# Products with the hidden-axis matrix spread over the running round, and stores handed to the DMA queue three ticks later

## The chip, the cores and the metric

The kernel runs on one core of a Trainium2 chip. The metric is the device time of one execution in microseconds (us), the median of several runs. The engines are called as the profile calls them: PE (matmuls) with PEld (its weight loads), DVE (vector), ACT (scalar), POOL (GpSimd), and SP, which here only issues DMAs.

## The reference

Two layers, each a spectral block and an attention block, on x of 2048 x 640 in float32. What the change touches is the spectral block:

```python
def _A_ref(x, dft_seq_re, dft_seq_im, dft_hid_re, dft_hid_im):
    a = einsum("bsd,ed->bse", x, dft_hid_re)
    b = einsum("bsd,ed->bse", x, dft_hid_im)
    return einsum("ts,bse->bte", dft_seq_re, a) - einsum("ts,bse->bte", dft_seq_im, b)

x = x + _A_ref(layernorm(x), ...)      # spectral
x = x + _B_ref(layernorm(x), ...)      # sliding-window attention, 32 heads, window 256
x = x + _A_ref(layernorm(x), ...)
x = x + _B_ref(layernorm(x), ...)
```

So each spectral block normalizes the rows, multiplies them with a 640-wide complex matrix (here `whid`), and multiplies the result with a 2048 x 2048 complex matrix (here `cmat`).

## The kernel before

Every float32 operand is split into a high and a low float16 part, and a product of two numbers is three matmuls (high x high, high x low, low x high). ACT writes a high part, DVE or POOL the low one, as the difference.

`spectral(layer, ...)` does one spectral block in four rounds (`NR = 4`). A round takes 512 of the 2048 input rows, in four tiles of 128 (`RS = 4`). For each of those tiles `z_stage(s)` forms the product with `whid`, which is called a whid stage here: four products of 15 matmuls each, every one into a bank of PSUM named `pf`, of which there are two (`new_f`, `bufs=2`). A bank is free again when DVE's subtractions (`minus`, L257) have read it. From the four products `parts`, `scaled` and `minus` make seven operands, kept in a buffer `zc` (or `early` for the first two stages of rounds 0 and 2).

Then the main part of the round: eight tiles of output (`j` = 0 to 7, `NJ = 8`), for each of which seven products (a Strassen-like scheme) of 12 matmuls are formed in banks `x`, `y` and `z`. `main_a(r, j)` does the first, `main_b(r, j)` four, `main_c(r, j)` the last two, which come after `main_a` of the next `j`. Their sums go into rows `res`, which are loaded (from the input in round 0, from `accd` in DRAM later) and stored to `accd`, or to `x2d` in the last round. DVE adds most of them from PSUM (`add`, L512); POOL adds three 320-column halves out of a work tile `pf` (L526, L536, L547). Four buffer pairs make `res` (`bufs=4`, two tiles of output).

The left operands come from `cmat`: `load_c` fetches one 1 MB block `cq` per `j`, two `j` ahead, `take_c` forms four sums `cs` on POOL (L478 to L481), and seven operands `cc` are split one per tick: `high` on ACT (L486), `low` on DVE (L489).

After each product stands a `tick()`: it emits the next pair of `splits` and one step of every generator in the list `side`. Such generators are `side_norm(s)` (load, normalize and split 128 rows of x for a whid stage of the next round, first layer only), `turn_x(s)` (transposes of those rows on PE), `b_max` (in round 0: 20 maxima on DVE, L618) and `b_split` (rounds 1 and 2: 15 chunks of the attention's weights, scaled on ACT, split on ACT and POOL at L660 to L663, stored to `bwd`). In the second layer the transposed rows are fetched from DRAM instead (`hidden.fetch`).

The stages of the next round stand partly inside the running one: after j = 6 and j = 7 stages 0 and 1; stages 2 and 3 follow at the start of the next round. `Projections()` loads the attention's weights (`big<-bwd`, two halves of 2400 KB) once the last stage is done, since they use the buffer of `whid`.

Every engine executes its own instructions in the order in which the framework put them; SP's DMAs are all issued from one queue, and an issue that has to wait for a buffer or for data holds those behind it.

Of the kernel before, what the change touches and what calls it, by code (L numbers as in the profile page):

```python
# [49 lines left out]
TURN_STEPS = 8  # L50
NORM_STEPS = (4, 9)
ROW_STEPS = 3
X_UP = 2.0 ** 10
C_UP = 2.0 ** 8
W_UP = 2.0 ** 13
# [6 lines left out]
def body(ctx: ExitStack, tc: tile.TileContext, x_in, cmat, whid, wqkv, wo, out):  # L62
# [108 lines left out]
    def load(out, in_):  # L171
        with ExitStack() as order:
            if in_turn[0] and loads:
                order.enter_context(tc.issue_after(loads[-1]))
            i = nc.sync.dma_start(out, in_)
        loads.append(i.ins)
# [26 lines left out]
    class Hidden:  # L203
# [21 lines left out]
        def stage(self, s, pool, new=new_f):  # L225

            w, xt = self.w, self.xt(s)
            if s % 8 < 2:
                zc = new_early()[:, :14 * HD].rearrange("p (m a d) -> p m a d", m=7, a=2)
            else:  # L230
                zc = pool.tile([P, 7, 2, HD], F16, tag="zc", name="zc", bufs=4)
            self.zc[s] = zc
            b11, b12, t1, t2, t3, t4 = (self.zf[:, k] for k in range(6))
            z = None

            def product(c, n):
                nonlocal z
                z = new()
                cs = slice(n * HD, (n + 1) * HD)
                k = 0  # L240
                for dt in range(ND):
                    for l, r in ((0, 0), (0, 1), (1, 0)):
                        self.last = matmul(z[:, :HD], xt[:, l, dt], w[:, r, c, dt, cs],
                                                     start=k == 0, stop=k == 14).ins
                        k += 1
                        yield 136
                z = z[:, :HD]

            def parts(m, f):
                nc.scalar.activation(zc[:, m, 0], f, AF.Copy)  # L250
                nc.gpsimd.tensor_tensor(zc[:, m, 1], f, zc[:, m, 0], op=OP.subtract)

            def scaled(o):
                nc.scalar.activation(o, z, AF.Copy, scale=Z_DOWN)

            def minus(o, f):
                nc.vector.scalar_tensor_tensor(o, z, Z_DOWN, f, op0=OP.mult, op1=OP.subtract)  # L257

            yield from product(0, 0)
            scaled(zc[:, B11, 0])  # L260
            scaled(b11)
            minus(zc[:, B11, 1], zc[:, B11, 0])
            yield 0
            yield from product(0, 1)
            scaled(b12)
            minus(t1, b11)
            parts(T1, t1)
            yield 0
            yield from product(1, 1)
            scaled(zc[:, B22, 0])  # L270
            minus(t2, t1)
            minus(t3, b12)
            minus(zc[:, B22, 1], zc[:, B22, 0])
            parts(T2, t2)
            parts(T3, t3)
            yield 0
            yield from product(1, 0)
            scaled(zc[:, B21, 0])
            minus(zc[:, B21, 1], zc[:, B21, 0])
            minus(t4, t2)  # L280
            parts(T4, t4)
            yield 0
# [62 lines left out]
    def spectral(layer, res_src, hidden, first):  # L345
        with ExitStack() as st:
# [30 lines left out]
            def drain():  # L377
                while splits or side:
                    tick()

            def load_w(n):
                c, dt = divmod(n, ND)
                f = sb.tile([P, D], F32, tag="xin", name="wst", bufs=NXIN)
                load(f, whid[c, :, dt])
                return f
# [125 lines left out]
            def add(o, z, f):  # L511
                marks["dve"] = nc.vector.scalar_tensor_tensor(o, z, Y_DOWN, f, op0=OP.mult, op1=OP.add).ins  # L512
# [4 lines left out]
            def main_a(r, j):  # L517
                res = [keep.tile([P, D], F32, tag="res", name="res", bufs=4) for k in range(2)]
                for k in range(2):
                    load(res[k], res_src[2 * j + k] if r == 0 else acc_d[2 * j + k])  # L520
                f = sb.tile([P, 3, HD], F32, tag="pf", name="pf", bufs=2)
                x = new_bank("x")
                cc = CC.pop((r, j))
                z = product(r, x, cc, 0, True, False)
                marks["act"] = nc.scalar.activation(f[:, 0], z, AF.Copy, scale=Y_DOWN).ins
                nc.gpsimd.tensor_tensor(res[1][:, lo], res[1][:, lo], f[:, 0], op=OP.add)  # L526
                tick()
                state[r, j] = [res, f, cc, x]

            def main_b(r, j):  # L530
                (x0, x1), f, cc, x = state[r, j]
                p1, u2, u3 = (f[:, k] for k in range(3))
                y = new_bank("y")
                z = product(r, y, cc, 1, True, False)
                add(u2, z, p1)
                nc.gpsimd.tensor_tensor(x0[:, hi], x0[:, hi], u2, op=OP.add)  # L536
                tick()
                z = product(r, x, cc, 2, False, True)
                add(x0[:, lo], z, x0[:, lo])
                tick()  # L540
                zb = new_bank("z")
                z = product(r, zb, cc, 4, True, False)
                add(x1[:, hi], z, x1[:, hi])
                tick()
                z = product(r, y, cc, 3, False, False)
                add(u3, z, p1)
                nc.gpsimd.tensor_tensor(x1[:, hi], x1[:, hi], u3, op=OP.add)  # L547
                tick()
                state[r, j] = [(x0, x1), cc, y, zb]

            def main_c(r, j):
                res, cc, y, zb = state.pop((r, j))
                x0, x1 = res
                z = product(r, zb, cc, 6, False, True)
                add(x0[:, hi], z, x0[:, hi])
                tick()
                z = product(r, y, cc, 5, False, True)
                add(x1[:, lo], z, x1[:, lo])
                last = r == NR - 1
                for k in range(2):  # L560
                    load((x2_d if last else acc_d)[2 * j + k], res[k])
                if last and j == 0:
                    side.append(chain(finish(0, 1), finish(1, 1)))
                tick()
# [87 lines left out]
            def b_split(n0, n1):  # L652
                fs = {n: b_chunk(n) for n in range(n0, n0 + 3)}
                for _ in range(4):
                    yield 1
                for n in range(n0, n1):
                    f = fs.pop(n)
                    t = keep.tile([P, 2, D], F16, tag="xto", name="bst", bufs=2)
                    hi, lo, sc = t[:, 0], t[:, 1], wsc[:, 0:1]
                    nc.scalar.activation(f, f, AF.Copy, scale=sc)  # L660
                    nc.scalar.activation(hi, f, AF.Copy)
                    yield 1
                    nc.gpsimd.tensor_tensor(lo, f, hi, op=OP.subtract)  # L663
                    cs = slice((n % 3) * D, (n % 3 + 1) * D)
                    for k in range(2):
                        load(bw_d[k][:, n // 3, cs], t[:, k])
                    if n + 3 < n1:
                        fs[n + 3] = b_chunk(n + 3)
                    for _ in range(5):
                        yield 1  # L670
# [22 lines left out]
                side.append(hidden.rest)  # L693
            load_c(0)
            for r in range(NR):
                for k in range(0 if r == 0 else 2, RS):
                    s = RS * r + k
                    if first:
                        if s == 1:
# [13 lines left out]
                            take_c(0)  # L713
                    if first or s > 1:
                        z_stage(s)
                if r == NR - 1:
                    proj = Projections()
                for j in range(NJ):
# [9 lines left out]
                    if r == NR - 1 and j == NJ - 1:  # L728
                        for _ in early_qk:
                            pass  # L730
                        for k in (1, 0):
                            proj.stack[k] = new_stack()
                            fill_stack(proj.stack[k], 0, k)
                    if first:
                        if r < NR - 1 and j in (3, 4):
                            side.append(side_norm(RS * (r + 1) + j - 3))
                        if r < NR - 1 and j == 5:
                            turn_x(RS * (r + 1))
                    if j == 0 and r == 0:
                        with behind():  # L740
                            while splits:
# [4 lines left out]
                    with ExitStack() as order:  # L746
# [3 lines left out]
                        if j:  # L750
                            main_c(r, j - 1)
                        main_b(r, j)
                    if r < NR - 1 and j >= NJ - 2:
                        k = j - (NJ - 2)
                        s = RS * (r + 1) + k
                        if first:
                            turned_x(s)
                            turn_x(s + 1, 2 if k == 0 else 0)
                            side.append(side_norm(s + 2))
                        else:  # L760
                            hidden.fetch(s)
                        z_stage(s)
                main_c(r, NJ - 1)
                if r == NR - 1:
                    drain()
# [542 lines left out]
```

## Time and profile before

| what | value |
| --- | --- |
| median of 3 runs | 2232.29 us (2230.44 to 2234.39) |
| profiled execution: span | 2233.0 us (nothing is shown around the span) |
| mean granted clock of PE | 0.991 |
| PE busy | 2122.0 us, 95% |
| DVE busy | 1646.4 us, 74% |
| POOL busy | 1391.6 us, 62% |
| ACT busy | 1288.8 us, 58% |
| DMA | 292.96 MB, mean 131 GB/s |

The first layer's spectral rounds begin at 53.75, 189.90, 332.60 and 472.30 us of the trace; a steady round of the second layer lies between 1320.00 and 1444.20. In a row of the timeline stand start, duration, engine, line, operation, `out<-in`, the count, and in brackets the idle time before it with what ended it. SPq is SP issuing a DMA; the transfer itself takes longer.

### The profile page before, as it was taken

To read this page: it belongs to the slowest core of one execution; us is meant where nothing else is said; L and a number is where in the kernel's file an instruction comes from. 1 tells how busy PE (TensorE), PEld (TensorE's weight loads), DVE (VectorE), ACT (ScalarE), POOL (GpSimd) and SP (SyncE) were. 2 spreads that over 40 slices of the span, in tenths; PEclk is the share of its full clock that TensorE was granted. 3 is DMA by queue.
4 is the path that set the end of the run, shared out by engine and by line. 5 is a ranking of instruction groups with operands and counts; after the bars stand their busy time and mean duration, and the time that the engine had idled before them with its cause. 6 is when DMAs were issued, how large, how long until landed. Compare 5 with 4: busy or idle time off the path is not lost.

```text
span 2233.0 us, 55112 instructions
## 1 busy us (share of the span) xinstructions
PE 2122.0 (95%) x21985; PEld 1494.7 (67%) x21985; DVE 1646.4 (74%) x3577; ACT 1288.8 (58%) x2155; POOL 1391.6 (62%) x1788
## 2 busy tenths in 40 slices
PE   7999899899999999999899999999998999999998
PEld 4767566676666766677566777777675666677765
DVE  8887958767677887887858758585767777777664
ACT  5434455443467777777754443434434777777775
POOL 5775968758355665566446858586674555566443
PEclk9999999999999999999999999999999999999999
DMA  6664646455533422333424536364743323332231
GB/s 252 219 224 143 229 138 225 156 188 175 142 79 67 103 71 73 94 91 84 134 79 160 193 127 212 110 207 145 256 133 96 83 63 85 93 87 59 57 80 37
DMA packets 187607, 292.96 MB, mean 131 GB/s; under 512 B 13908, under 2 KB 120660, under 8 KB 178004
## 3 DMA queue, kind: packets, MB, share of 16 engines
q1 hardware_dynamic: 186772, 288.77, 42.1%
q8 instruction: 172, 2.82, 0.5%
q14 instruction: 87, 0.71, 0.1%
q10 hardware_dynamic: 576, 0.66, 0.1%
HBM read 202.51 MB, written 86.87 MB: 130 GB/s over the span
## 4 chain that ended last, share of the span: by engine, by line
PE 59%; DVE 12%; DMA 4%; issue 3%; POOL 2%; ACT 2%; SPq 1%; DVEq 0%; POOLq 0%; ACTq 0%
PE pf L115 24%; PE pv L115 8%; PE y L115 7%; PE sp L115 5%; PE x L115 5%; PE z L115 5%; PE tp L115 3%; DVE m L1062 3%; DVE sp L1058 2%; PE pt L115 2%; DVE cc L489 1%; DMA res<-accd 1%; DMA x2d<-res 1%; PE acc L115 1%; DMA qs<-qkd 1%
## 5 line engine op out<-in xcount | busy, mean ns | idle before, releaser
L115 PEld LDWEIGHTS <-cc 128*128 128x128 f16 x5376 | 525.1, 98 | 215.6 <-issue 10.6
L1106 ACT ACTIVATE ptq<-tp,shift,alpha 128x768 f32<-128x768 f32 (+2 forms) x512 | 486.2, 950 | 163.6 <-PE tp L115 155.6
L115 PEld LDWEIGHTS <-big 128*128 128x128 f16 x4320 | 408.5, 98 | 151.9 <-issue 40.5
L1062 DVE TENSOR_REDUCE m<-sp 128x2 f32<-128x512 f32 (+1 forms) x512 | 345.1, 674 | 16.8
L1058 DVE COPY_PREDICATED sp<-mask,sp 128x256 f32<-128x256 int32 x448 | 190.8, 426 | 188.2 <-PE sp L115 176.5
L115 PE MATMUL pf<-early,big 128*128 128x256 f16 x2400 | 313.9, 274 | 2.9 <-ACT early L401 2.5
L1111 POOL TENSOR_SCALAR_AFFINE_SELECT ptq<-ptq 128x512 f32<-128x512 f32 x224 | 145.5, 649 | 265.4 <-ACT ptq L1106 261.7
L486 ACT ACTIVATE cc<-cs 128x512 f16<-128x512 f32 x256 | 151.6, 623 | 254.6 <-POOL cs L478 124.1
L115 PE MATMUL y<-zc,cc 128*128 128x320 f16 x1728 | 263.8, 300 | 2.4 <-DVE pf L512 2.4
L115 PE MATMUL pf<-big 128*128 128x320 f16 x1680 | 245.6, 304 | 19.2 <-DVE zc L257 9.3
L489 DVE SCALAR_TENSOR_TENSOR cc<-cs,cc 128x512 f16<-128x512 f32 x256 | 255.2, 1012 | 9.9 <-ACT cc L486 9.7
L489 DVE SCALAR_TENSOR_TENSOR cc<-cq,cc 128x512 f16<-128x512 f32 x192 | 198.7, 1036 | 0.0
L1113 POOL TENSOR_SCALAR_AFFINE_SELECT ptq<-ptq 128x512 f32<-128x512 f32 x256 | 163.9, 640 | 43.1 <-ACT ptq L1106 43.1
L115 PE MATMUL pv<-ptq,v 128*32 128x128 f32 (+1 forms) x3840 | 183.7, 330 | 0.0
L115 PE MATMUL z<-zc,cc 128*128 128x320 f16 x1152 | 178.5, 299 | 2.0 <-ACT cc L486 1.0
L115 PE MATMUL x<-zc,cc 128*128 128x320 f16 x1152 | 179.7, 299 | 0.0
L115 PE MATMUL sp<-ks,qs 62*128 62x256 f16 (+1 forms) x1792 | 153.6, 248 | 20.8 <-DVE m L1062 18.6
L115 PE MATMUL pf<-big,early 128*128 128x320 f16 x960 | 162.3, 301 | 6.4 <-DVE x L883 6.4
L1083 ACT ACTIVATE qs<-pt 2x512 f16<-2x512 f16 x224 | 131.0, 585 | 42.7 <-PE pt L115 40.0
L115 PE MATMUL tp<-qs,ks 62*128 62x128 f16 x2688 | 150.1, 217 | 3.2 <-ACT ptq L1106 2.7
L115 PE MATMUL pf<-bo,ot 128*128 128x320 f16 x840 | 147.2, 302 | 3.3 <-DVE ot L956 2.8
L167 POOL TENSOR_TENSOR xs<-lny,xs 128x640 f16<-128x640 f32 x63 | 94.2, 1497 | 83.3 <-ACT xs L166 82.6
(144 smaller groups left out, 3525.3 us busy)
## 6 DMA issues: line engine op xcount, KB each, us to landing
cq<-in_cmat_dram SPq DMA_DIRECT2D x64, 1024.0 KB
accd<-res SPq DMA_DIRECT2D x96, 320.0 KB
res<-accd SPq DMA_DIRECT2D x96, 320.0 KB
x<-x2d SPq DMA_DIRECT2D x64, 320.0 KB
qkd<-early SPq DMA_DIRECT2D x160, 128.0 KB
ks<-qkd SPq DMA_DIRECT2D x108, 160.0 KB
qs<-qkd SPq DMA_DIRECT2D x84, 160.0 KB
x2d<-res SPq DMA_DIRECT2D x32, 320.0 KB
```

Of the source, the lines that this page charges most:

```text
L115: i = getattr(nc.tensor, what)(*args, **kw)
L167: eng.tensor_tensor(lo, y, hi, op=OP.subtract)
L486: nc.scalar.activation(cc[m][:, 0], f, AF.Copy, scale=C_UP)
L489: nc.vector.scalar_tensor_tensor(cc[m][:, 1], f, C_UP, cc[m][:, 0], op0=OP.mult, op1=OP.subtract)
L1058: nc.vector.copy_predicated(sp[:, :, 2 * P:3 * P], mask[:, None, :].to_broadcast([P, 2, P]), far)
L1062: topped[0] = nc.vector.tensor_reduce(TOP[g // 4][:, g % 4], sp[:, :, c0:3 * P], axis=AX.X, op=OP.max).ins
L1083: nc.scalar.activation(o, handed[n][rs].rearrange("r (i p) t -> r i p t", i=2), AF.Copy)
L1106: nc.scalar.activation(q[:, h:h + 2, a0 + first:a0 + 3], tp[:, :, first * P:3 * P].rearrange("p a (b c) -> p a b c", c=P), AF.Sigmoid, bia ...
L1111: nc.gpsimd.affine_select(out=q[:, :, a0], in_=q[:, :, a0], pattern=[[0, 4], [-1, P]], base=0, channel_multiplier=1, compare_op=OP.is_gt, ...
L1113: ins = nc.gpsimd.affine_select(out=q[:, :, a0 + 2], in_=q[:, :, a0 + 2], pattern=[[0, 4], [1, P]], base=0, channel_multiplier=-1, compare ...
```

## The change

It does four things. All four stages of the next round stand in the running round, after j = 1, 3, 5 and 6, and the norms and transposes that feed them start earlier (norms at j = 0, 1, 2, 3). The stores of `res` to `accd` and of the split weights to `bwd` are emitted by a generator `later`, three ticks after the place where they stood. The work tile `pf` has two thirds instead of three. Six `zc` buffers replace four; a smaller descriptor area makes room.

```diff
+STORE_LAG = 3
+STAGES = (1, 3, 5, 6)
...
-                zc = pool.tile([P, 7, 2, HD], F16, tag="zc", name="zc", bufs=4)
+                zc = pool.tile([P, 7, 2, HD], F16, tag="zc", name="zc", bufs=6)
...
+            def later(pairs):
+                for _ in range(STORE_LAG):
+                    yield 1
+                for dst, src in pairs:
+                    load(dst, src)
+                yield 1
...
-                f = sb.tile([P, 3, HD], F32, tag="pf", name="pf", bufs=2)
+                f = sb.tile([P, 2, HD], F32, tag="pf", name="pf", bufs=2)
...
-                add(u3, z, p1)
-                nc.gpsimd.tensor_tensor(x1[:, hi], x1[:, hi], u3, op=OP.add)
+                add(p1, z, p1)
+                nc.gpsimd.tensor_tensor(x1[:, hi], x1[:, hi], p1, op=OP.add)
...
-                for k in range(2):
-                    load((x2_d if last else acc_d)[2 * j + k], res[k])
+                pairs = [((x2_d if last else acc_d)[2 * j + k], res[k]) for k in range(2)]
+                if last:
+                    for dst, src in pairs:
+                        load(dst, src)
+                else:
+                    side.append(later(pairs))
...
-                    for k in range(2):
-                        load(bw_d[k][:, n // 3, cs], t[:, k])
+                    side.append(later([(bw_d[k][:, n // 3, cs], t[:, k]) for k in range(2)]))
...
-                for k in range(0 if r == 0 else 2, RS):
+                for k in range(RS if r == 0 else 0):
...
+                    if not first and s > 1:
+                        hidden.fetch(s + 2)
...
-                    if first:
-                        if r < NR - 1 and j in (3, 4):
-                            side.append(side_norm(RS * (r + 1) + j - 3))
-                        if r < NR - 1 and j == 5:
-                            turn_x(RS * (r + 1))
+                    if first and r < NR - 1:
+                        for k, at in enumerate(STAGES):
+                            if j == max(at - 3, k):
+                                side.append(side_norm(RS * (r + 1) + k))
+                        if j == STAGES[0] - 1:
+                            turn_x(RS * (r + 1), 4)
...
-                    if r < NR - 1 and j >= NJ - 2:
-                        k = j - (NJ - 2)
+                    if r < NR - 1 and j in STAGES:
+                        k = STAGES.index(j)
                         s = RS * (r + 1) + k
                         if first:
                             turned_x(s)
-                            turn_x(s + 1, 2 if k == 0 else 0)
-                            side.append(side_norm(s + 2))
-                        else:
-                            hidden.fetch(s)
+                            if k < RS - 1:
+                                turn_x(s + 1, 2)
                         z_stage(s)
+                        if not first and s + 2 < NT:
+                            hidden.fetch(s + 2)
...
-    nc = _bacc.Bacc("TRN2", target_bir_lowering=False, num_devices=1)
+    nc = _bacc.Bacc("TRN2", target_bir_lowering=False, num_devices=1, dynamic_dma_scratch_size=1024)
```

The lines of the kernel move by 2 to 13: L257 becomes L259, L489 becomes L498, L512 becomes L521, L399 becomes L408, L526 becomes L535, L536 becomes L545, L547 becomes L556, L478 to L481 become L487 to L490, L175 becomes L177.

DVE, first layer, round 2, between the last addition of the main tile ahead of a stage (`pf<-y`) and the first subtraction of that stage (`zc<-pf`). Before, at the stage after j = 6 (`cc` with `cs` or `cq` are the low parts of the left operands, `lnst` the norm's statistics):

```order
L512 SCALAR_TENSOR_TENSOR pf_4850<-y_4901,pf_4850 128x320
L489 SCALAR_TENSOR_TENSOR cc_4950<-cs_4839,cc_4950 128x512
L489 SCALAR_TENSOR_TENSOR cc_4967<-cs_4839,cc_4967 128x512
L489 SCALAR_TENSOR_TENSOR cc_4990<-cs_4839,cc_4990 128x512
L128 BN_STATS lnst_5075<-xin_4992 128x6
L489 SCALAR_TENSOR_TENSOR cc_5084<-cq_4837,cc_5084 128x512
L257 SCALAR_TENSOR_TENSOR zc_4969<-pf_4970,zc_4969 128x320
```

Now, at the round's first stage, after j = 1 (`lnt` are the norm's small steps, the copy brings transposed rows out of PSUM):

```order
L521 SCALAR_TENSOR_TENSOR pf_4095<-y_4161,pf_4095 128x320
L498 SCALAR_TENSOR_TENSOR cc_4220<-cs_4084,cc_4220 128x512
L408 COPY big_166<-pf_4256 128x640
L142 TENSOR_SCALAR lnt_4232<-lnt_4232 128x1
L498 SCALAR_TENSOR_TENSOR cc_4254<-cs_4084,cc_4254 128x512
L143 TENSOR_SCALAR lnt_4232<-lnt_4232 128x1
L498 SCALAR_TENSOR_TENSOR cc_4291<-cs_4084,cc_4291 128x512
L142 TENSOR_SCALAR lnt_4232<-lnt_4232 128x1
L498 SCALAR_TENSOR_TENSOR cc_4391<-cq_4082,cc_4391 128x512
L143 TENSOR_SCALAR lnt_4232<-lnt_4232 128x1
L147 TENSOR_SCALAR lnt_4232<-lnmv_4182,lnt_4232 128x1
L259 SCALAR_TENSOR_TENSOR zc_4270<-pf_4271,zc_4270 128x320
```

The four lows stay, and a copy and five norm steps have come between. At the third stage, after j = 5, two lows are left (the fourth stage reads the same, and the second has norm steps besides two lows):

```order
L521 SCALAR_TENSOR_TENSOR res_4959<-z_5049,res_4959 128x320
L498 SCALAR_TENSOR_TENSOR cc_5047<-cs_4951,cc_5047 128x512
L521 SCALAR_TENSOR_TENSOR pf_4962<-y_5015,pf_4962 128x320
L498 SCALAR_TENSOR_TENSOR cc_5064<-cs_4951,cc_5064 128x512
L498 SCALAR_TENSOR_TENSOR cc_5189<-cq_4949,cc_5189 128x512
L259 SCALAR_TENSOR_TENSOR zc_5083<-pf_5084,zc_5083 128x320
```

The other lows of that tile have moved behind the stage's subtractions or ahead of the last addition.

SP, first layer, from the end of round 2 into round 3, the last one (`big` the attention's weights, `cq` a block of `cmat`, `res` from `accd` rows of the last round, 0 and 1 those of its first tile). Before:

```order
L175 DMA accd12_123<-res_4846 128x640
L175 DMA accd13_124<-res_4847 128x640
L175 DMA cq_5562<-in_cmat_dram 128x2048
L175 DMA res_5571<-accd0_111 128x640
L175 DMA res_5572<-accd1_112 128x640
L175 DMA accd14_125<-res_5086 128x640
L175 DMA res_5671<-accd2_113 128x640
L175 DMA accd15_126<-res_5087 128x640
L175 DMA res_5672<-accd3_114 128x640
L175 DMA big_5559<-bwd0_145 128x9600
L175 DMA big_5559<-bwd1_146 128x9600
L175 DMA cq_5662<-in_cmat_dram 128x2048
```

Now:

```order
L177 DMA accd12_123<-res_5191 128x640
L177 DMA accd13_124<-res_5192 128x640
L177 DMA big_5557<-bwd0_145 128x9600
L177 DMA big_5557<-bwd1_146 128x9600
L177 DMA cq_5560<-in_cmat_dram 128x2048
L177 DMA res_5569<-accd0_111 128x640
L177 DMA res_5570<-accd1_112 128x640
L177 DMA accd14_125<-res_5408 128x640
L177 DMA accd15_126<-res_5409 128x640
L177 DMA cq_5662<-in_cmat_dram 128x2048
```

The two halves of the weights have moved ahead of the rows of the last round's first tiles.

More of the change, by code (lines that the diff above doesn't have):

```diff
@@ L531, in main_b @@
                 (x0, x1), f, cc, x = state[r, j]
-                p1, u2, u3 = (f[:, k] for k in range(3))
+                p1, u2 = (f[:, k] for k in range(2))
                 y = new_bank("y")
```

## The prediction

> **What bounds the kernel now.** I read the page first, then the clock of the core, then a table by stages, the waits of the matmul engine, and the timeline around each wait.
>
> ```profile
> span 2233.0 us, 55112 instructions
> PE 2122.0 (95%) x21985; PEld 1494.7 (67%) x21985; DVE 1646.4 (74%) x3577; ACT 1288.8 (58%) x2155; POOL 1391.6 (62%) x1788
> ```
>
> PE is busy for 95% of the span, so the change can only win back PE's idle time, or add to it. The attention phases keep every engine's order, so only the spectral phases count. The table takes rounds 0, 1 and 2 of the first layer, each cut in two where its first whid stage begins, and then one steady round of the second layer. Columns are length, PE busy and count, the same for PE's weight loads, DVE, ACT, POOL, then the granted clock, DMA share and GB/s.
>
> ```profile
> 53.75:132.95 79.20, 77.65 (x577) 55.77 (x575) 70.78 (x120) 32.53 (x60) 63.46 (x47) 1.00 0.67 226
> 132.95:189.90 56.95, 53.07 (x392) 37.48 (x390) 38.17 (x85) 25.66 (x54) 31.85 (x31) 0.97 0.49 158
> 189.90:268.20 78.30, 75.83 (x565) 54.57 (x563) 70.75 (x121) 37.88 (x68) 66.43 (x49) 1.00 0.63 211
> 268.20:332.60 64.40, 55.11 (x392) 38.52 (x390) 35.87 (x76) 31.63 (x63) 43.20 (x38) 0.92 0.45 151
> 332.60:412.50 79.90, 76.33 (x564) 54.38 (x562) 69.57 (x109) 39.86 (x71) 69.55 (x52) 1.00 0.65 215
> 412.50:472.30 59.80, 54.28 (x392) 38.00 (x390) 36.36 (x77) 25.74 (x54) 33.90 (x32) 0.94 0.27 92
> 1320.00:1396.60 76.60, 76.60 (x566) 55.18 (x565) 61.42 (x87) 30.01 (x58) 62.10 (x47) 1.00 0.57 190
> 1396.60:1444.20 47.60, 47.47 (x350) 34.05 (x349) 23.86 (x47) 19.31 (x44) 26.03 (x27) 1.00 0.36 121
> ```
>
> A second-layer round takes 76.60 + 47.60 = 124.2 us at full clock: 916 matmuls, 0.136 us each, so a product of 12 takes 1.63 and one of 15 takes 2.04. A first-layer round has 41 matmuls more (565 + 392 against 566 + 350), transposes of 128 columns instead of 320: 41 x 0.136 x 0.4 = 2.2 us. It could take 126.4 and takes 136.15, 142.70 and 139.70. It loses 9.7, 16.3 and 13.3, together **39.3 us**. That is what the change can reach. The second layer has nothing to give. Where the loss sits, by what PE waited for between 100 and 480 us (total, times, longest):
>
> ```profile
> PE pf L115 <- DVE zc L257: 9.3, 4, 5.3
> PE pf L115 <- DVE early L257: 9.3, 2, 7.3
> PE pf L115 <- POOL xs L167: 4.3, 2, 2.5
> ```
>
> The third product of a stage wants the bank that DVE's first subtraction (L257) frees. The timeline shows why DVE comes late, in round 1 and, last two rows, in the second layer:
>
> ```profile
> 266.58 1.79 PE L115 MATMUL y<-zc,cc 128*128 128x320 f16 x12
> 267.61 1.35 DVE L489 SCALAR_TENSOR_TENSOR cc<-cq,cc 128x512 f16<-128x512 f32 x1
> 270.56 0.48 DVE L512 SCALAR_TENSOR_TENSOR pf<-y,pf 128x320 f32<-128x320 f32 x1
> 272.47 4.14 DVE L489 SCALAR_TENSOR_TENSOR cc<-cs,cc 128x512 f16<-128x512 f32 x3 [1.43 <-ACT cc L486]
> 273.09 1.71 POOL L481 TENSOR_TENSOR cs<-cq,cs 128x512 f32<-128x512 f32 x1
> 277.72 0.83 ACT L660 ACTIVATE wst<-wst,wsc 128x640 f32<-128x640 f32 x1 [1.74 <-DMA wst<-in_wqkv_dram]
> 279.23 0.49 DVE L257 SCALAR_TENSOR_TENSOR early<-pf,early 128x320 f16<-128x320 f32 x1 [1.35 <-ACT big L254]
> 279.77 4.16 PE L115 MATMUL pf<-big 128*128 128x320 f16 x15 [7.32 <-DVE early L257]
> ...
> 1270.46 1.61 POOL L481 TENSOR_TENSOR cs<-cq,cs 128x512 f32<-128x512 f32 x1
> 1272.48 8.58 PE L115 MATMUL pf<-big 128*128 128x320 f16 x60
> ```
>
> PE ends its last main product at 268.37, but DVE adds it only at 270.56: it is 2.2 us behind, because norms and splits of matrix C share it. Then its low parts (L489) wait for ACT's high parts, those for POOL's L481, which ends 6.6 us into the stage. Once more DVE waits for ACT, which was held by a chunk of weights that came late. In the second layer L481 ends before the stage begins, and the stage runs through in one piece.
>
> **The waits cost clock too.** Rows of windows that begin where PE resumes (length, PE busy, granted clock, DMA share, GB/s):
>
> ```profile
> 279.77:283.93 4.16, 4.16 (x17) 0.50 0.24 100
> 139.79:143.04 3.25, 3.25 (x16) 0.65 0.75 233
> 303.74:306.30 2.56, 2.56 (x13) 0.67 0.10 36
> ...
> 139.79 3.25 PE L115 MATMUL pf<-big 128*128 128x320 f16 x15 [2.61 <-DVE zc L257]
> 303.74 2.55 PE L115 MATMUL pf<-big 128*128 128x320 f16 x12 [1.97 <-DVE early L257]
> ```
>
> After 7.32 us of waiting 15 matmuls took 4.16 instead of 2.04, after 2.61 they took 3.25. So I add 1.2 to a wait of 2 to 4 us and 2.1 to a longer one. [...]
>
> **The change, part by part.** In each round all four stages now follow a main tile (j = 1, 3, 5, 6), so none runs at a round's start any more. I price what stands on DVE between the last main addition and the first subtraction, by these groups (busy, mean ns):
>
> ```profile
> L489 DVE SCALAR_TENSOR_TENSOR cc<-cs,cc 128x512 f16<-128x512 f32 x96 | 101.3, 1067 | 5.6 <-ACT cc L486 5.5
> L140 DVE TENSOR_SCALAR lnt<-lnt 128x1 f32<-128x1 f32 x36 | 9.7, 270 | 0.9
> L141 DVE TENSOR_SCALAR lnt<-lnt 128x1 f32<-128x1 f32 x36 | 7.6, 210 | 0.8
> L399 DVE COPY big<-pf 128x640 f16<-128x640 f16 x12 | 5.9, 489 | 14.8 <-PE pf L115 14.8
> L618 DVE TENSOR_REDUCE wmax<-wst 128x1 f32<-128x640 f32 x20 | 16.2, 808 | 0.7 <-DMA wst<-in_wo_dram 0.7
> ```
>
> First stage (order rows of the change): four lows 4.28, the copy 0.49, five norm steps 2 x 0.27 + 3 x 0.21 = 1.17, in all 5.94. With a hop of about 0.2 (my estimate), the addition 0.48 and the subtraction 0.49 DVE is done 7.1 us after the last main product. Two stage products cover 4.07. The wait is **3.0 plus DVE's lag**. Second stage: two lows and five norm steps, 3.35, so 0.45 plus the lag. Third and fourth: two lows, 2.14, done at 3.3, so 0.8 us of lag are absorbed. In round 0 one or two maxima (0.81) come into each of them. The highs no longer hold DVE from the second stage on, since three of POOL's four sums of C now run during the stage before, and the loads of weight chunks no longer stand behind a store that waits for POOL.
>
> For the lag I take 0.5 to 1 us: less than 2.2, as the norms are spread over seven tiles and every stage gives DVE a pause. Rounds 1 and 2 then pay 3.7 + 1.2 for the first stage, 1.2 for the second, 0.3 each for the others, and 1.3 for transposes and late rows, 8.0 each. Round 0 pays 2.8 more for maxima, 10.8. That is 26.8 against 39.3: **12.5 saved**. [...]
>
> **Stores handed over later.** A steady tile's rows on SP, and POOL's first use of the loaded rows:
>
> ```profile
> 1343.65 1.92 SPq L175 DMA_DIRECT2D accd<-res  x2
> 1346.21 1.92 SPq L175 DMA_DIRECT2D res<-accd  x2
> 1350.65 0.33 SPq L175 DMA_DIRECT2D cq<-in_cmat_dram  x1
> 1342.00 1.02 POOL L526 TENSOR_TENSOR res<-res,pf 128x320 f32<-128x320 f32 x1 [0.25 <-ACT pf L525]
> ```
>
> The loads went out 1346.21 to 1348.13 and are used a tile (11.41) after 1342.00, at 1353.4: over 5 us between. In the new order the 1 MB of C goes ahead of them. At the rate of the next rows it takes about 3 us, so POOL finds them some 2 us before use. I book nothing, and the 1.3 above holds what the first layer's busier queue may cost. At the last round it is worse: `res` of its first tile now stands behind both halves of the next weights and C.
>
> ```profile
> 475.28 0.85 SPq L175 DMA_DIRECT2D big<-bwd  x2
> 477.11 0.33 SPq L175 DMA_DIRECT2D cq<-in_cmat_dram  x1
> 484.53 11.13 DMA x2d<-res
> ```
>
> From 475.28 to the end of that store at 495.66, 20.4 us, the queue moved two halves of weights, C and two stores. Now the weights go out about 6 us before the last round begins, as their buffer is free a tile earlier, and `res` lands 12 to 14 us into it. DVE's addition to it, and the lows behind, stop there; PE can run on until about 12.2 (five products of the first tile, one and a half of the next). I take 3.5 per layer, less 1 for waits that the same queue causes there now: 2 x 2.5 = **5 lost**, between -3 and +11.
>
> Sum: -12.5 + 5 = -7.5. The profiled span is 2232.95 and the median 2232.29, and the page shows nothing around the span, so the sum is taken off the median: **2225 us**. What else changes (six buffers, one work slot fewer, a smaller descriptor area) stands in no wait of the trace; a slot fewer could bind only if u2 were still unread when the next tile begins, seven products later, and I book 0.
>
> **The rivals.** *DVE never catches up (slower).* The place is the first subtraction of each stage. The busy DVE halves (70.8 of 79.2) speak for it, the second layer (no lag at 61.4 of 76.6) against. With a lag of 2.2 the four stages cost 5.2 + 2.1, 2.7 + 1.2 and twice 1.4, 14 a round; with transposes, late rows and maxima 46, or 7 more than now; with the last rounds 12: **2244**. It decides from a lag of about 1.5 us. Chance 0.20. *Gains are eaten by loads (no change).* `res` stops each layer's last round by 5.5, as POOL's sums for the third tile queue behind it too, and half a microsecond goes at each of the first layer's tiles without a stage: -12.5 + 11 + 0.5 = **2231**. Chance 0.20. *The stages become as smooth as in the second layer.* If ready highs let the lag vanish and the first wait stay under 2 us, a round loses 3.5 to 4: -27 + 5 = **2210**, and 2205 if the last rounds are free. Chance 0.15. The forecast keeps 0.45.
>
> **The numbers.** A difference of 0.2% (4.5 us) is what this measurement can tell. Of the forecast's 0.45, 0.38 lies under 2227.8 and 0.07 within; with 0.15 of the smooth case faster has 0.53. Same takes 0.07 and 0.15 of the loads' case, 0.22; slower the lag's 0.20 and 0.05 of the loads, 0.25. The range runs from the smooth case's 2205 past the lag's 2244 to 2252, for a lag of 2.7.
>
> **What would show it.** Right: rounds 0 to 2 at 137, 134.5 and 134.5 us; a wait for L259 of 3 to 4 us at each first stage and under 1 at the third and fourth; none for first stages at a round's end. Wrong: waits over 2 us at third stages (the lag), PE waiting over 4 us for DVE 12 us into the last rounds (the loads), or rounds that stay at 136 to 143.

## The result: no gain, and where it went

The changed kernel took 2235.66 us (median of 14 runs, 2229.91 to 2239.35), the kernel before 2232.05 beside it (14 runs). The ratio is 1.001, 95% interval 1.0 to 1.0019: no change, or at most 4 us slower. The forecast was 2225. The runs of either kernel spread over 10 us, and the traced one of the changed kernel, 2229.91, is the fastest of its 14, so its trace flatters it. A second trace stands below.

The page after, the same two rows as of before:

```profile
span 2228.1 us, 55112 instructions
PE 2115.0 (95%) x21985; PEld 1490.9 (67%) x21985; DVE 1615.2 (72%) x3577; ACT 1283.3 (58%) x2155; POOL 1376.9 (62%) x1788
```

Rounds 0, 1 and 2 of the first layer, by stage (length, PE, PEld, DVE, ACT, POOL, clock, DMA share, GB/s), and what PE waited for in them (total, times, longest):

```profile
53.44:189.12 135.68, 128.90 (x953) 92.02 (x951) 101.97 (x204) 57.20 (x115) 89.05 (x76) 0.99 0.53 189
189.12:325.59 136.47, 128.91 (x955) 91.94 (x953) 99.62 (x196) 67.42 (x128) 103.77 (x85) 0.99 0.53 186
325.59:457.81 132.22, 127.24 (x954) 91.28 (x952) 95.75 (x184) 65.69 (x126) 104.36 (x84) 1.00 0.52 185
...
PE pf L117 <- ACT xs L168: 8.1, 3, 2.8
PE pf L117 <- DVE zc L259: 4.4, 3, 2.8
PE pf L117 <- DVE early L259: 4.4, 1, 4.4
PE pf L117 <- POOL xs L169: 1.0, 1, 1.0
```

The three rounds together take 404.4 us, where before they took 136.15 + 142.70 + 139.70 = 418.6, or 416.8 between the marks of the table below (the end of each round's first main product). The difference is in the cuts of before: 53.75 is where round 0's first product begins, while at 189.90, 332.60 and 472.30 PE had already done the round's first product, amid the last stage, so the cuts hold one product more (969 matmuls in round 0, 957 in round 1). So 12.4 us were won there. The last rounds of the two layers took 10.1 us longer in this trace and 14.2 in the second one. First at the start of round 3, first layer:

```profile
448.93 0.32 SPq L177 DMA_DIRECT2D accd<-res  x1
449.34 0.88 SPq L177 DMA_DIRECT2D big<-bwd  x2
450.27 0.45 SPq L177 DMA_DIRECT2D cq<-in_cmat_dram  x1
450.82 1.24 SPq L177 DMA_DIRECT2D res<-accd  x2
...
469.53 0.49 DVE L521 SCALAR_TENSOR_TENSOR res<-x,res 128x320 f32<-128x320 f32 x1 [6.75 <-issue]
471.44 1.79 PE L117 MATMUL z<-zc,cc 128*128 128x320 f16 x12 [0.93 <-DVE res L521]
...
484.03 0.49 DVE L521 SCALAR_TENSOR_TENSOR pf<-y,pf 128x320 f32<-128x320 f32 x1 [1.57 <-POOL res L535]
484.57 3.42 PE L117 MATMUL y<-zc,cc 128*128 128x320 f16 x24 [1.55 <-DVE pf L521]
```

The weights go out 8.5 us before the round starts at 457.81, the rows of its first tile behind them, and DVE can add to those rows only at 469.53, 11.7 into the round. The profile calls the idle time "issue"; that it ends when the rows are there is read from the queue, and a run below shows it. The last two rows, from the third tile, are the first sign of something else: DVE's sum into the work tile waits for POOL's L535, and PE for that sum. Then at the end of the same round, the last tile:

```profile
566.56 2.02 SPq L177 DMA_DIRECT2D res<-accd  x2
570.33 1.79 PE L117 MATMUL y<-zc,cc 128*128 128x320 f16 x12
574.57 0.49 DVE L521 SCALAR_TENSOR_TENSOR res<-x,res 128x320 f32<-128x320 f32 x1 [7.25 <-DMA res<-accd]
575.34 0.49 DVE L521 SCALAR_TENSOR_TENSOR res<-z,res 128x320 f32<-128x320 f32 x1 [0.28 <-DMA res<-accd]
575.89 1.79 PE L117 MATMUL z<-zc,cc 128*128 128x320 f16 x12 [3.76 <-DVE res L521]
```

That wait was not in the prediction. Before, PE had other work there, although the rows came as late (here the second layer; their first use is 4.8 us after the fourth product begins, and 4.2 in the rows above). In the first layer PE's `z` product waits 0.21 us in the kernel before and 3.76 in the changed one.

```profile
1679.54 1.79 PE L115 MATMUL y<-zc,cc 128*128 128x320 f16 x12 [0.58 <-DVE pf L512]
1681.16 2.20 PE L115 MATMUL pf<-big,early 128*128 128x320 f16 x15
1681.94 0.49 DVE L512 SCALAR_TENSOR_TENSOR res<-x,res 128x320 f32<-128x320 f32 x1 [2.45 <-DMA res<-accd]
1683.25 1.79 PE L115 MATMUL z<-zc,cc 128*128 128x320 f16 x12
```

The order of the two kernels says how. Before, DVE's sum of the fourth product (`pf<-y`) stood ahead of the two sums that wait for rows; now it stands behind them, and PE's `y` product and fifteen projection matmuls behind `z`.

### The profile page after: what moved, and what is told of

Read it like the earlier page. It is cut to its first block, busy times and chain, and to the rows that moved or that the text cites. A ratio compares the mean times of both kernels' runs of the same rounds, so it can differ in the third digit from the quotient of the medians.

```text
span 2228.1 us, 55112 instructions
## 1 busy us (share of the span) xinstructions
PE 2115.0 (95%) x21985; PEld 1490.9 (67%) x21985; DVE 1615.2 (72%) x3577; ACT 1283.3 (58%) x2155; POOL 1376.9 (62%) x1788
## 4 chain that ended last, share of the span: by engine, by line
PE 70%; DVE 17%; issue 4%; DMA 4%; ACT 2%; POOL 2%; SPq 1%; DVEq 0%; ACTq 0%; POOLq 0%
PE pf L117 27%; PE y L117 10%; PE pv L117 8%; PE z L117 7%; PE x L117 7%; PE sp L117 5%; DVE cc L498 4%; PE tp L117 3%; DVE m L1077 3%; DVE sp L1073 2%; PE pt L117 2%; DVE res L521 1%; DMA res<-accd 1%; DVE lnt L142 1%; SPq L177 1%
## 5 line engine op out<-in xcount | busy, mean ns | idle before, releaser
L117 PEld LDWEIGHTS <-big 128*128 128x128 f16 x4320 | 407.4, 98 | 139.9 <-issue 30.6
L495 ACT ACTIVATE cc<-cs 128x512 f16<-128x512 f32 x256 | 149.4, 622 | 141.0 <-POOL cs L488 61.9
L498 DVE SCALAR_TENSOR_TENSOR cc<-cs,cc 128x512 f16<-128x512 f32 x256 | 224.4, 883 | 0.0
L498 DVE SCALAR_TENSOR_TENSOR cc<-cq,cc 128x512 f16<-128x512 f32 x192 | 203.3, 1059 | 0.0
L117 PE MATMUL z<-zc,cc 128*128 128x320 f16 x1152 | 179.7, 301 | 10.2 <-DVE res L521 10.1
L556 POOL TENSOR_TENSOR res<-res,pf 128x320 f32<-128x320 f32 x64 | 77.7, 1213 | 127.0 <-DVE pf L521 113.1
## 6 DMA issues: line engine op xcount, KB each, us to landing
qkd<-early SPq DMA_DIRECT2D x160, 128.0 KB
```

What stands on the lines that cost most here:

```text
L117: i = getattr(nc.tensor, what)(*args, **kw)
L495: nc.scalar.activation(cc[m][:, 0], f, AF.Copy, scale=C_UP)
L498: nc.vector.scalar_tensor_tensor(cc[m][:, 1], f, C_UP, cc[m][:, 0], op0=OP.mult, op1=OP.subtract)
L556: nc.gpsimd.tensor_tensor(x1[:, hi], x1[:, hi], p1, op=OP.add)
```

## The experiments

All are compared with the kernel before on the same chip; not all on one chip, so two variants are best compared by their ratios. The table gives medians, the ratio to before with its interval, and from one trace each the lengths in us of four parts: rounds 0 to 2 and the last round of each layer. They run from ACT's first read of a round's first product to the next such mark; a last round ends at attention's first row of the group `ptq<-tp` on ACT. The text cuts a last round in two at the mark of its sixth tile, up to which PE has done the same 445 or 446 matmuls in every kernel here. Single traces differ: rounds 0 to 2 of the first layer run in the same order in the changed kernel, again, late_weights, rows_first, adds_last and own_slot, and took 404.4 to 409.0 us.

| kernel | median | ratio (95%) | layer 1: rounds 0-2 | last | layer 2: rounds 0-2 | last |
| --- | --- | --- | --- | --- | --- | --- |
| before | 2232.05 | | 416.8 | 132.7 | 376.8 | 125.9 |
| changed | 2235.66 | 1.0010 (1.0-1.0019) | 404.4 | 134.5 | 377.3 | 134.2 |
| again | 2236.97 | 1.0016 (1.0003-1.0029) | 404.4 | 136.6 | 377.3 | 136.2 |
| spread_now | 2232.56 | 0.9994 (0.9981-1.0007) | 404.4 | 134.5 | 377.3 | 135.6 |
| lag_only | 2231.42 | 0.9996 (0.9985-1.0008) | 415.7 | 130.7 | 376.8 | 125.9 |
| late_weights | 2229.66 | 0.9983 (0.9971-0.9995) | 405.7 | 134.4 | 377.4 | 129.7 |
| rows_first | 2222.43 | 0.9958 (0.9946-0.9970) | 407.4 | 130.8 | 377.3 | 128.5 |
| both_fixes | 2218.45 | 0.9936 (0.9923-0.9949) | 407.2 | 129.4 | 377.4 | 124.5 |
| before_rows | 2229.12 | 0.9981 (0.9973-0.9990) | 415.7 | 130.0 | 376.8 | 124.3 |
| both_2456 | 2223.25 | 0.9956 (0.9943-0.9968) | 411.0 | 127.4 | 376.7 | 124.8 |
| adds_last | 2238.24 | 1.0016 (1.0006-1.0027) | 406.5 | 136.7 | 377.3 | 136.2 |
| spread_rows | 2217.14 | 0.9927 (0.9914-0.9939) | 405.3 | 129.5 | 377.4 | 126.1 |
| all_three | 2216.94 | 0.9926 (0.9913-0.9940) | 406.2 | 128.0 | 377.4 | 126.1 |
| own_slot | 2225.41 | 0.9968 (0.9958-0.9979) | 409.0 | 133.7 | 377.4 | 131.2 |
| two_thirds | 2240.18 | 1.0031 (1.0018-1.0044) | 417.4 | 137.4 | 376.9 | 130.2 |
| spread_slot | 2230.62 | 0.9992 (0.9979-1.0004) | 404.3 | 135.5 | 377.3 | 130.3 |
| spread_rows_slot | 2226.22 | 0.9970 (0.9959-0.9981) | 406.1 | 133.8 | 377.3 | 128.8 |

**Again**: the changed kernel, unaltered.

> The changed kernel once more, to see a second execution of it. Theory A (the gain of the first layer's rounds is given back in the last rounds of both layers): rounds 0 to 2 again end 12 to 13 us earlier than before, the last rounds again take 10 us more in sum, and the median is that of the changed kernel, 2232 to 2238. Theory B (the stage spreading gains nothing on most executions; the profiled one was lucky): rounds 0 to 2 gain less than 6 us here.

The first layer's gain is the same to a tenth; theory B falls. The last rounds vary: 272.8 us here, 268.7 in the first trace, 258.6 before. Most executions took longer than either trace.

**Spread_now**: stages spread, stores at once.

```diff
-                    side.append(later(pairs))
+                for k in range(2):
+                    load((x2_d if last else acc_d)[2 * j + k], res[k])
```

> The changed kernel with the stores handed over at once, as before; the stages stay spread. Here the next weights stand behind the rows of the last round's first tiles on SP again. Theory A: the early stall of both last rounds goes (7 us), the first layer keeps at least 8 of its 12.5 us: 2226 to 2230. Rival C (the late stores are what freed the weight chunks and the highs, and so the first layer's gain): the first layer's gain falls under 5 us, the median stays at 2232 to 2236.

The gain is kept in full, so rival C falls: the late stores bring the first layer nothing. But the median missed the forecast of theory A: only the starts of the last rounds improved (to their sixth tile 63.2 and 63.3 us, the changed kernel 65.6 and 65.9, before 64.8 and 61.8). Their ends stayed long: 71.4 and 72.2 from there, before 67.8 and 64.1.

**Lag_only**: the kernel before with `later` for its stores.

> The kernel before with only the stores handed over three ticks later; stages where they were. Theory A: the first stalls of rounds 1 and 2 shrink by what the weight chunks held (1 to 3 us each), the last rounds stay as before, since the weights still wait for the last stages: 2228 to 2232. Rival C: most of the first layer's gain is here, 2222 to 2226. If late stores cost by themselves: 2234 or more.

The median lies where theory A had it, but not for its reason: the waits ahead of the first stages of rounds 1 and 2 did not shrink. They were 7.32 and 5.26 us and are 7.64 and 5.25, and ACT still waits there for a chunk of weights, 1.94 us where it waited 1.74. Rounds 0 to 2 are 1.1 us shorter, less than traces of one order differ.

```profile
278.95 0.83 ACT L672 ACTIVATE wst<-wst,wsc 128x640 f32<-128x640 f32 x1 [1.94 <-DMA wst<-in_wqkv_dram]
281.01 4.16 PE L116 MATMUL pf<-big 128*128 128x320 f16 x15 [7.64 <-DVE early L258]
```

**Late_weights**:

```diff
-                if r == NR - 1:
-                    proj = Projections()
...
                         main_a(r, j)
+                        if r == NR - 1 and j == 1:
+                            proj = Projections()
```

> The changed kernel with the load of the attention's weights handed to SP behind the rows of the last round's second tile. Theory A: the stall some 12 us into both last rounds goes, 3 to 4 us each, so 2227 to 2230 where the changed kernel has 2235. If that stall is covered by something later (the rows of the last tile, which wait behind the loads for attention), the end of the last round moves by less than 2 us in each layer: 2232 to 2235.

6.0 us below the changed kernel, so the early weights cost about that. The traces agree: to the sixth tile 63.7 and 61.9 us, 1.9 and 4.0 less than in the changed kernel. The 6.7 us in which DVE waited at the start are gone.

**Rows_first**: the loads for attention's first product moved behind `main_a` of the last tile; **both_fixes**: this and late weights.

```diff
-                        for k in (1, 0):
-                            proj.stack[k] = new_stack()
-                            fill_stack(proj.stack[k], 0, k)
...
                         main_a(r, j)
+                        if r == NR - 1 and j == NJ - 1:
+                            for k in (1, 0):
+                                proj.stack[k] = new_stack()
+                                fill_stack(proj.stack[k], 0, k)
```

> The changed kernel with the loads of the last tile's rows ahead of the fourteen loads for attention on SP, the weights still early. Theory A, second part (at the end of each last round PE stops 4 us for those rows, because the new order puts a main product on them ahead of fifteen projection matmuls): 3 to 5 us back in each layer, 2227 to 2231 where the changed kernel has 2236. If that stop only waits for the loads behind it (attention cannot start before them anyway), 2234 to 2237.

> The changed kernel with both: the weights' load behind the second tile's rows, and the last tile's rows ahead of attention's loads. Theory A: all that the last rounds took is back, and the 12 to 13 us of the first layer's rounds stay: 2219 to 2225. If the loads for attention are now late by as much, 2227 to 2230.

From early rows alone 13.2 us are back by the medians and 11.6 by the ratios, more than the 6 to 10 expected. With both corrections the gain of the first layer shows at last, half a microsecond better than expected.

**Before_rows**: the same move in the kernel before.

> The kernel before with the loads of the last tile's rows ahead of attention's loads, nothing else. Theory A: its PE has fifteen projection matmuls to do while those rows come, so at most 2 us per layer are to be had: 2228 to 2232. If the rows' load holds the last round by itself in both kernels, it gains as much as in the changed one, 4 us a layer: 2223 to 2226.

Only 4 us, where the changed kernel got 13. So the change itself had made the rows' late arrival dear.

**Both_2456**: `STAGES = (2, 4, 5, 6)` on top of both corrections.

> Both corrections, and the stages after j = 2, 4, 5 and 6 instead of 1, 3, 5 and 6, so that the norm ahead of a round's first stage has a tile more. Theory A, third part (what the first layer still loses is the norm that comes late for the transposes, 2.8 us in each of three rounds, and lows ahead of the second stage): the transposes' waits go, 5 to 9 us less than with both corrections alone. Rival: the norm's steps then stand ahead of the second stage, and the wait only moves: within 2 us of it.

Theory A's third part falls. The rival was right that nothing is won, but it had the time within 2 us of both corrections alone, and the median is 4.8 higher; in the traces rounds 0 to 2 take 3.8 us longer. PE still waits three times for the high part of the normed rows:

```profile
PE pf L117 <- ACT xs L168: 8.6, 3, 3.3
PE pf L117 <- DVE zc L259: 7.9, 4, 4.0
PE pf L117 <- DVE early L259: 4.9, 2, 4.7
```

**Adds_last**: in the last tile of the last rounds DVE's sums and the two main products are put back into the old order by hand; the projection matmuls stay behind. The part on DVE's sums:

```diff
+                if end:
+                    with tc.issue_after(marks["dve"]):
+                        add(x0[:, lo], z2, x0[:, lo])
+                        add(x1[:, hi], z4, x1[:, hi])
```

> The changed kernel with a forced order for the last tile of each last round only: DVE's addition to the work tile ahead of the two additions that wait for the rows, and the main product in bank y ahead of the one in bank z. The loads stay as late as in the changed kernel. Theory A, second part (the moved order took away PE's cover of 1.63 us for the product and 2.04 for fifteen projection matmuls): this gives the product back, so the wait at the end falls by 1.6 us in each layer, 2232 to 2234. Rival: the order is no part of it, the rows are just late: 2235 to 2238.

The second part of theory A, as I had put it, falls: 2238.24, at its rival's end of 2238. The trace tells what it missed. DVE, POOL and PE in the last tile:

```profile
576.06 0.86 POOL L545 TENSOR_TENSOR res<-res,pf 128x320 f32<-128x320 f32 x1 [12.35 <-DMA res<-accd]
576.87 0.86 POOL L535 TENSOR_TENSOR res<-res,pf 128x320 f32<-128x320 f32 x1
577.76 0.49 DVE L521 SCALAR_TENSOR_TENSOR pf<-y,pf 128x320 f32<-128x320 f32 x1 [4.54 <-POOL res L535]
578.31 3.36 PE L117 MATMUL y<-zc,cc 128*128 128x320 f16 x12 [3.98 <-DVE pf L521]
```

The sum of the fourth product now writes the third of the work tile that POOL's L535 still has to read, and POOL waits for the rows. It is the pair that stood at the third tile of the changed kernel above. The order was the scheduler's answer to that, not the cause. **Theory S**: the dropped third of the work tile ties PE to the rows' arrival.

**Two_thirds** drops that third in the kernel before; **own_slot** gives the changed kernel a separate buffer in the last rounds:

```diff
-                add(p1, z, p1)
-                nc.gpsimd.tensor_tensor(x1[:, hi], x1[:, hi], p1, op=OP.add)
+                u3 = p1 if r < NR - 1 else sb.tile([P, D], F32, tag="xin", name="u3", bufs=NXIN)[:, lo]
+                add(u3, z, p1)
+                nc.gpsimd.tensor_tensor(x1[:, hi], x1[:, hi], u3, op=OP.add)
```

> The kernel before with the work tile of two thirds instead of three, nothing else. Theory S: the last rounds lose what they lose in the changed kernel at their end, 3 to 5 us a layer, and 0 to 2 at their start: 2238 to 2244, slower. Rival: 2231 to 2235, the same.

> The changed kernel, with a buffer of its own (a free one of the input's) for the fourth product's sum in the last rounds; loads and stores as in the changed kernel. Theory S (the dropped third of the work tile makes DVE's fourth addition wait until POOL has read the slot, and POOL waits for the rows; so PE's next products wait for the rows too): the end of each last round gets back 3 to 5 us, 2226 to 2230 where the changed kernel has 2236. Rival (the rows are late, whatever the slot): 2234 to 2238.

Both came as theory S said, own_slot half a microsecond lower. Two_thirds alone is 7 us slower than before (4 to 10 by its interval), its last rounds 4.7 and 4.3 longer, its PE order at the end that of the changed kernel. Own_slot is 9 to 10 us faster than the changed kernel, and the order of PE and DVE at the end is that of before again. Two_thirds, then own_slot, last tile of the first layer:

```profile
587.89 0.49 DVE L512 SCALAR_TENSOR_TENSOR res<-x,res 128x320 f32<-128x320 f32 x1 [8.03 <-DMA res<-accd]
589.21 3.09 PE L115 MATMUL z<-zc,cc 128*128 128x320 f16 x11 [4.55 <-DVE res L512]
```

```profile
576.86 0.49 DVE L521 SCALAR_TENSOR_TENSOR u<-y,pf 128x320 f32<-128x320 f32 x1 [4.84 <-PE y L117]
577.40 1.79 PE L117 MATMUL y<-zc,cc 128*128 128x320 f16 x12 [0.58 <-DVE u L521]
579.03 2.20 PE L117 MATMUL pf<-big,early 128*128 128x320 f16 x15
580.89 0.49 DVE L521 SCALAR_TENSOR_TENSOR res<-x,res 128x320 f32<-128x320 f32 x1 [3.54 <-DMA res<-accd]
```

In both DVE stands waiting for the same rows; in the second the sum is done before, and PE has 27 matmuls to do meanwhile.

**Spread_rows**: spread_now and early rows. **All_three**: both_fixes and the forced order. **Spread_slot**: spread_now and the separate buffer. **Spread_rows_slot**: both of these.

> Stages spread as in the changed kernel, all stores handed over at once as before, and the last tile's rows ahead of attention's loads. Theory A: the late stores brought the first layer nothing and only let the weights go ahead of the rows, so this is as good as the changed kernel with both corrections: 2216 to 2222. Rival: the late stores are worth something once the last rounds are mended: 2223 to 2227.

> The changed kernel with both corrections of the loads and the forced order of the last tile. Theory A: with the rows in time the order no longer matters, so within 2 us of the kernel with both corrections: 2216 to 2221. If the order costs by itself, 3 us less: 2213 to 2216.

> Stages spread, all stores at once as before, and a buffer of its own for the fourth product's sum in the last rounds; the loads are left where they are. Theory S with theory A: nothing of the change's costs is left, the first layer's 12 us stay: 2219 to 2223. Rival: the last tile's rows still come late and cost as much as without the buffer, 2229 to 2233.

> As the run before it, with the last tile's rows ahead of attention's loads as well. Theory S: with the rows in time the slot matters little, so within 2 us of the run with spread stages, stores at once and early rows (2217): 2215 to 2218. If the two add up: 2210 to 2214.

The first two came as expected, and they are the versions to keep: 0.7% faster than before, spread_rows with the least code. The last two missed, and spread_slot met its rival's 2229 to 2233: by the ratios it is 0.4 us faster than spread_now, nothing clear of noise. Its trace shows two effects that oppose each other. The ends of the last rounds shrink by 4.1 and 8.2 us, to 67.3 and 64.1, those of the kernel before. But their starts grow by 5.1 and 2.9 (68.2 and 66.2 us to the sixth tile, 63.2 and 63.3 in spread_now), and PE waits 2.9 us for ACT's high part:

```profile
PE y L117 <- ACT cc L495: 2.9, 1, 2.9
...
482.69 0.49 DVE L521 SCALAR_TENSOR_TENSOR res<-z,res 128x320 f32<-128x320 f32 x1 [1.08 <-PE z L117]
483.70 0.48 DVE L521 SCALAR_TENSOR_TENSOR u<-y,pf 128x320 f32<-128x320 f32 x1
484.26 1.24 POOL L557 TENSOR_TENSOR res<-res,u 128x320 f32<-128x320 f32 x1 [3.20 <-DVE u L521]
```

On DVE the sum into the separate buffer stands behind the sum of a later product there (at 483.70, behind `res<-z` at 482.69; in spread_now it stands ahead of it), POOL's L557 waits 3.2 us for it, and POOL's sums of C and ACT's high parts come behind that. Why the order came out so, no run shows.

So theory S is shown for the ends of the last rounds. With late rows they take 66.2 to 68.3 us (first layer) and 64.1 to 65.2 (second) where the sum has a place of its own, and 68.9 to 72.6 and 67.7 to 72.2 where it has not (adds_last among these). With early rows they take 65.6 and 62.5 either way (rows_first, both_fixes, both_2456, before_rows, spread_rows, spread_rows_slot; all_three, with its forced order, 66.4 and 63.4). The separate buffer is not the best cure, early rows are.

## Why the prediction was wrong, step by step

**The first layer's rounds: near in sum, partly by luck, and not in its terms.** Forecast were 137, 134.5 and 134.5 us, measured 135.7, 136.5 and 132.2. That the 12.4 us saved are so close to the 12.5 forecast is partly chance: the 39.3 that I called reachable counts one product of 12 matmuls too many, 1.8 us in the cuts, and the rounds came out 1.6 us shorter than forecast. With the spread of traces the saving is 8 to 12 us (own_slot's 409.0 to 404.4). The wait of 3.7 us for the first subtraction of a round didn't come: PE stops earlier, 2.6 to 2.8 us three times, for the high part of the normed rows that the transposes want; that DVE catches up meanwhile is likely, but no run shows it. The wait came at the second stage instead, which I had priced at 1.2: 2.8 us in round 0, 4.4 in round 1 and 1.0 in round 2. Third and fourth stages wait under 1, as forecast. The hop of 0.2 from a product's end to DVE, called my estimate, is what the trace before shows in the second layer: PE begins the next product at 1269.22, and DVE, which stood idle 0.16 us for the product before, starts its sum at 1269.42. The lag rival fell. (Its 46 also leaves out the 2.8 for maxima that it names.)

**The last rounds' start: right mechanism.** Forecast 2.5 us lost per layer, measured 0.7 and 4.1 to the sixth tile, 4.9 together against 5. Taking it away brought 6.0 in the median and 5.9 in the traces. (The products that I listed as PE's work until 12.2 us are six and a half, 10.6 us; PE stopped at 12.7.)

**The work slot: the step that failed.** I wrote that a slot fewer could bind only if u2 were still unread when the next tile begins, and booked 0. The slot that was reused is not u2 but p1, which POOL reads for rows that come last, and it binds within the tile. Cost by itself, in the kernel before: 7 us. The order of DVE at the end of the last rounds, where the sum stands behind two others, shows it; the prediction had weighed their starts alone.

Sum: -12.4 from the spread stages, + 6 for early weights, + 7 for the slot, about 0; measured + 3.6 in the medians, + 2.2 by the ratio. The 2 to 3 us that are left are open. The costs need not simply add, since the slot also binds at the third tile, where the weights make the rows late; and no run takes back the six `zc` buffers or the smaller descriptor area alone. The rival in which loads eat the gain named the place (late rows in the last rounds) and nearly the time, 2231, but not the slot that makes them cost so much. Its time is partly luck too: half a microsecond at each of the twelve tiles without a stage would be 6, and its sum has 0.5.

## What to carry to other kernels

Where a buffer is saved by writing a result over an operand, ask which engine still has to read that operand and what it waits for: here a vector sum inherited a DMA's lateness through POOL (in adds_last POOL waited 12.35 us for the rows, DVE's sum 4.54 for POOL and PE 3.98 for the sum), and the scheduler spread it over PE's order. When work is moved off a boundary, look at what becomes free earlier and goes out earlier, here two loads of 2400 KB ahead of the first rows of the next round on one queue. Compare the new order also where the diff does nothing, above all where a loop ends.

## What was unexpected of the hardware

The clock doesn't follow the length of a wait alone. Five windows of the changed kernel that begin where PE resumes (length, PE busy, clock, DMA share, GB/s), and two of the waits before them:

```profile
74.15:77.50 3.35, 3.35 (x31) 1.00 0.98 367
209.98:213.00 3.02, 3.02 (x29) 1.00 0.96 336
346.65:349.30 2.65, 2.08 (x17) 1.00 0.92 282
116.02:119.30 3.28, 3.28 (x15) 0.60 0.45 144
253.38:257.00 3.62, 3.62 (x16) 0.55 0.45 142
...
346.65 0.45 PE L117 MATMUL pf<-idh,xs 128*128 128x128 f16 x5 [2.83 <-ACT xs L168]
116.02 0.57 PE L117 MATMUL pf<-big 128*128 128x320 f16 x3 [2.83 <-DVE zc L259]
```

After one wait of 2.83 us PE ran at full clock, after another of 2.83 at 0.60. The waits before the other three windows were 2.62 and 2.63 us, with full clock behind them, and 4.38, with 0.55. What decides between the two equal waits, no run here shows. So what I added to a wait, 1.2 us or 2.1 for a longer one, was paid after two of five: there 15 matmuls took 3.28 us and 16 took 3.62, where 0.136 each makes 2.04 and 2.18.
